# Fewer and larger first input transfers in a fused attention and soft-MoE kernel

## Chip, cores and metric

The kernel runs on one core of one Trainium2 chip. The metric is the device time of one launch in microseconds; lower is better.

## What is computed

An attention read between 512 tokens and 32 states for each of 8 batches and 8 heads (in both directions) is followed by a soft mixture of 8 experts with 4 slots each over all 4608 rows. Everything is float32. The reference, cut to its core:

```python
scores = scale * np.matmul(x, state.transpose(0, 1, 3, 2))       # x (8, 8, 512, 64), state (8, 8, 32, 64)
a = softmax(scores);   xread = np.matmul(a, state)
scores2 = scale * np.matmul(state, x.transpose(0, 1, 3, 2))
a2 = softmax(scores2); sread = np.matmul(a2, x)
x = np.concatenate([xread, sread], axis=2)                        # rows of 512 columns, 4608 of them
logits = x @ phi                                                  # phi (512, 32)
d = softmax(logits, axis=0); slot_input = d.T @ x
h = np.maximum(slot_input[e] @ w1[e], 0.0); slot_out[e] = h @ w2[e]
c = softmax(logits, axis=1); out = c @ slot_out
```

## The kernel before

One function, `attention_soft_moe`, writes the program. All loads and stores go through DMA queues, almost all through that of SyncE (SP). The tokens of one batch are 1 MB, `x0` to `x7`; the states (`stT_sb`, 512 KB) and the gate `phi_sb` (64 KB) are small; the weights `w1` and `w2` are 32 MB and follow behind the tokens on the same queue.

The first lines of the function issue the loads (lines 84 to 101). Batch 0 comes in four transfers of 256 KB, one for each pair of heads `g`: pieces 0 and 2 are issued by SP, pieces 1 and 3 by ScalarE (ACT). Then SP issues a quarter of the states (`st0`, batches 0 and 1), batch 1 in two halves, the other three quarters of the states (`st1`), `phi`, batches 2 to 7, and the weights. The semaphores that tell of a landing are eight, used in turn over all transfers of both queues, so a transfer may be issued only when the one eight before it has landed.

The order of the compute work is written out by hand in the table `ORDER` (lines 30 to 56), a list of steps such as `X.0.1`; each step is a small function of the same name. Those that matter here, for batch b:

- `W.n` (line 649): matmuls of the identity with itself, n columns, that keep TensorE (PE) busy while the first data is on its way.
- `X.b.g` (line 229): four PE transposes of 128x128 of token piece g into PSUM. `xe` (ACT, line 234) or `xd` (VectorE, DVE, line 239) copies the result to SBUF with the scale.
- `S.b` (line 248): 16 score matmuls from the transposed tokens and the states.
- `q`, `m1`, `sub`, `x1`, `l1`, `m2`, `e2` and so on: the softmaxes in both directions, on DVE, ACT and GpSimd (POOL).
- `G.i` (line 212): products of states and gate for two batches. Its operand `phi_bd` is built by two POOL copies from `phi_sb` (line 204), ahead of all other POOL work of the batches.

The table begins `W.512 W.256 X.0.1 xd.0.1 X.0.0 xd.0.0 X.0.2 xe.0.2 X.0.3 xe.0.3 S.0 X.1.0 m2.0.1 X.1.2 X.1.1 ... G.1 ... X.1.3 E.0.1 ... G.2 S.1`. Each engine works its share of the table in order. After the attention part (to about 76 us) come the expert matmuls with `w1` (line 700) and `w2` (line 763) and the output matmuls (lines 799 and 822), whose results ACT and DVE copy to SBUF and SP stores in 11 transfers.

The states' buffer is used a second time: when the last step that reads the states is through, `load_part` (line 686) puts a part of `w2` into it.

Of the kernel before, what the change touches and what calls it, by code (L numbers as in the profile page):

```python
# [8 lines left out]
F32 = mybir.dt.float32  # L9
# [6 lines left out]
P = 128  # L16
B = 8
S = 512
NS = 32
D = 64  # L20
E = 8
F = 1024
NJ = S // P
# [37 lines left out]


@with_exitstack
def attention_soft_moe(ctx: ExitStack, tc: tile.TileContext, x0, x1, x, st0, st1, phi, w1, w2a, w2b, out_x, out_s):

# [3 lines left out]
    nc = tc.nc  # L71
    pe, act, dve, pool = nc.tensor, nc.scalar, nc.vector, nc.gpsimd

    cp = ctx.enter_context(tc.tile_pool(name="const", bufs=1))
# [2 lines left out]
    pairs = ctx.enter_context(tc.tile_pool(name="pairs", bufs=NPAIR))  # L77


    one = ctx.enter_context(tc.tile_pool(name="one", bufs=1))  # L80
    stT_sb = one.tile([P, 4, 2, 2, 2, NS], F32, tag="one", name="stT_sb")
    phi_sb = cp.tile([P, 4, NS], F32, name="phi_sb")
    xb = []
    for b in range(B):
        t = big.tile([P, 4, NJ, 2 * D], F32, tag="big", name=f"x{b}")
        if b == 0:
            for i in range(4):
                v = x0[i].rearrange("p (g j c) -> p g j c", g=1, j=NJ)
                (act if i % 2 else nc.sync).dma_start(t[:, 1 * i : 1 * i + 1], v)
        elif b == 1:  # L90
            for i in range(2):
                v = x1[i].rearrange("p (g j c) -> p g j c", g=2, j=NJ)
                nc.sync.dma_start(t[:, 2 * i : 2 * i + 2], v)
        else:
            nc.sync.dma_start(t, x[b - 2].rearrange("p (g j c) -> p g j c", g=4, j=NJ))
        xb.append(t)
        if b == 0:
            nc.sync.dma_start(stT_sb[:, 0:1], st0)
        if b == 1:
            nc.sync.dma_start(stT_sb[:, 1:4], st1)  # L100
            nc.sync.dma_start(phi_sb, phi)


    w1t, w2t = {}, {}
# [34 lines left out]
    def load_part(t, k, e, ft):  # L139
        n = t.shape[1] // 256  # L140
        t = t.rearrange("p (k f) -> p k f", k=n)
        nc.sync.dma_start(t, w2a[e // 2, k][:, e % 2, ft : ft + n])
        for i in range(n):
            w2t[2, k, e, ft + i] = t[:, i]
# [32 lines left out]
    with ExitStack() as actx:  # L177
# [15 lines left out]
        def half(name):  # L193
            return wk.tile([P, S], F32, tag="h", name=name, bufs=NH)
# [487 lines left out]
        for i, step in enumerate(order):  # L682
            name, *args = step.split(".")
            steps[name](*map(int, args))
            if i == states_read:
                load_part(one.tile([P, F], F32, tag="one", name=f"w2_{k1}_{e1}"), k1, e1, 0)
            if i == halves_had:
                for k, e in ((k1, e1 + 1), (k2, e2)):
                    for ft in (0, 2):
                        load_part(half(f"w2_{k}_{e}_{ft}"), k, e, ft)  # L690
# [42 lines left out]
        c = [half(f"c{i}") for i in range(3)]  # L733
        c = [v[:, 0 : t.shape[1]].rearrange("p (t n) -> p t n", n=NS) for v, t in zip(c, c_t)]
# [213 lines left out]
```

## Time and profile before

| | us |
|---|---|
| median of 3 runs | 130.0 |
| lowest and highest run | 129.94, 130.71 |
| span of the profiled execution | 128.2 |

The profile tells the span of the profiled execution, from its first instruction to its last, and not that execution's device time. The difference to the median of the runs, 130.0 - 128.2 = 1.8 us, is taken as what lies around the span. All times inside the profile count from the start of the span.

In the rows, "PEld" is the loading of weights into PE, which overlaps the matmuls ("PE"); "SPq" and "ACTq" are DMA issues by SyncE and ScalarE. In brackets stands how long the engine sat idle before a group and what ended that. Matmul ends are modelled, so "PE busy" is an upper bound.

### The profile page before, as it was taken

The page shows a single profiled execution, that of the slowest core. Times are in us where ns is not written, and L with a number is a line of the kernel's source. Part 1 is how long each engine was busy: PE and PEld are TensorE (multiplying, and loading weights), DVE is VectorE, ACT ScalarE, POOL GpSimd, SP SyncE. Part 2 cuts the span into 40 slices and gives each one's busy share as a digit, 9 for nine tenths or more (in the row PEclk, how much of TensorE's full clock was granted, in tenths as well). Part 3 has the DMA queues.
Part 4 walks back from the last instruction along what each step waited for, and adds up shares of the span by engine and source line. Part 5 has one row for each costly group of instructions (what it writes and reads, how often), then busy time and mean ns, then how long its engine had stood idle before and what let it go on. Part 6 is the DMA issues. An engine that isn't in the chain of part 4 may idle for free.

```text
span 128.2 us, 4700 instructions
## 1 busy us (share of the span) xinstructions
PE 117.7 (92%) x1992; PEld 81.7 (64%) x1992; DVE 86.7 (68%) x194; ACT 76.9 (60%) x189; POOL 44.8 (35%) x63
## 2 busy tenths in 40 slices
PE   5999999999999999999999999999999999998600
PEld 2857686789795869768767769953465655575200
DVE  2329999999999999999985669019830356442600
ACT  4039999999999999999965711310100436645600
POOL 3004366391947467467882105703500000000000
PEclk9999999999999999999999999999999999999965
DMA  4999999999999999999999999999999989999992
GB/s 125 377 407 430 424 427 422 424 422 424 422 419 422 427 419 429 419 429 417 429 417 435 412 420 402 459 440 409 412 445 445 389 366 417 429 406 422 385 423 100
DMA packets 8373, 51.74 MB, mean 404 GB/s; under 512 B 928, under 2 KB 1184, under 8 KB 3360
## 3 DMA queue, kind: packets, MB, share of 16 engines
q1 hardware_dynamic: 8064, 50.93, 95.5%
q10 hardware_dynamic: 288, 0.52, 1.1%
q8 instruction: 15, 0.25, 0.7%
q14 instruction: 6, 0.05, 0.1%
HBM read 42.53 MB, written 8.91 MB: 401 GB/s over the span
## 4 chain that ended last, share of the span: by engine, by line
PE 71%; DVE 9%; DMA 7%; ACT 5%; issue 1%; POOL 0%; ACTq 0%; DVEq 0%; POOLq 0%
PE so_ps L763 12%; PE h_ps L700 11%; PE xt_ps L229 8%; PE o L799 7%; PE sc L248 5%; DMA phi_sb<-phi_in 5%; PE eT_ps L312 4%; PE sr_ps L346 4%; PE an_ps L312 3%; PE lt L381 3%; DMA x<-x_in 3%; PE t_ps L506 2%; DVE sums L277 2%; DVE q L261 2%; DVE m L266 1%
## 5 line engine op out<-in xcount | busy, mean ns | idle before, releaser
L270 POOL TENSOR_TENSOR q<-q,m 128x512 f32<-128x512 f32 x16 | 16.8, 1050 | 15.7 <-DVE m L266 7.3
L234 ACT ACTIVATE xt<-xt_ps 128x512 f32<-128x512 f32 x30 | 17.9, 618 | 5.9 <-PE xt_ps L229 5.7
L229 PE MATMUL xt_ps<-ident,x 128*128 128x128 f32 x128 | 19.3, 293 | 0.0
L288 POOL TENSOR_TENSOR q<-q,rr 128x512 f32<-128x512 f32 x16 | 16.5, 1051 | 5.1 <-DVE rr L283 3.6
L229 PEld LDWEIGHTS xt_ps<-ident,x 128*128 128x128 f32 x128 | 15.5, 151 | 3.1 <-PE sc L248 0.8
L763 PE MATMUL so_ps<-w,h_m 128*32 128x128 f32 (+1 forms) x384 | 15.7, 310 | 0.0
L763 PEld LDWEIGHTS so_ps<-w,h_m 128*32 128x32 f32 x384 | 10.7, 110 | 7.4 <-issue 4.6
L809 DVE COPY out<-o 128x512 f32<-128x512 f32 x14 | 9.2, 688 | 9.0 <-PE o L799 8.8
L700 PE MATMUL h_ps<-w,si_m 128*32 128x512 f32 x128 | 14.4, 594 | 0.1
L299 DVE TENSOR_REDUCE nm<-sc 128x1 f32<-128x512 f32 x16 | 10.6, 670 | 2.7 <-PE sc L248 2.7
L808 ACT COPY out<-o 128x512 f32<-128x512 f32 x14 | 7.7, 588 | 6.8 <-PE o L799 6.7
L700 PEld LDWEIGHTS h_ps<-w,si_m 128*32 128x32 f32 x128 | 9.1, 110 | 3.9 <-issue 2.9
L304 ACT ACTIVATE e<-sc,nm 128x512 f32<-128x512 f32 x16 | 11.3, 711 | 0.4 <-DVE nm L299 0.3
L261 DVE STREAM_TRANSPOSE q<-sc 128x512 f32<-128x512 f32 x16 | 11.1, 695 | 0.1
L293 DVE STREAM_TRANSPOSE aT<-q 128x512 f32<-128x512 f32 x16 | 10.9, 689 | 0.3 <-POOL q L288 0.2
L266 DVE TENSOR_REDUCE m<-q 128x16 f32<-128x512 f32 x16 | 10.5, 659 | 0.0
L277 DVE TENSOR_REDUCE sums<-q 128x16 f32<-128x512 f32 x16 | 10.4, 664 | 0.1
L273 ACT ACTIVATE q<-q 128x512 f32<-128x512 f32 x16 | 10.4, 650 | 0.1
L346 PE MATMUL sr_ps<-x,eT 128*32 128x64 f32 x512 | 10.4, 220 | 0.0
L312 PE MATMUL eT_ps<-ident,e 128*128 128x128 f32 x64 | 9.8, 279 | 0.0
L248 PE MATMUL sc<-xt,stT_sb 64*32 64x512 f32 x128 | 9.8, 601 | 0.0
L346 PEld LDWEIGHTS sr_ps<-x,eT 128*32 128x32 f32 x512 | 8.6, 110 | 1.3 <-issue 0.8
(124 smaller groups left out, 186.1 us busy)
## 6 DMA issues: line engine op xcount, KB each, us to landing
w<-w_in SPq DMA_DIRECT2D x16, 1024.0 KB, 19.7
w<-w2b_in SPq DMA_DIRECT2D x4, 2048.0 KB, 14.7
out_x<-out SPq DMA_DIRECT2D x7, 1024.0 KB, 6.0
x<-x_in SPq DMA_DIRECT2D x6, 1024.0 KB, 13.5
w<-w2a_in SPq DMA_DIRECT2D x6, 1024.0 KB, 19.4
x<-x_in SPq DMA_DIRECT2D x2, 512.0 KB, 5.9
w<-w2a_in SPq DMA_DIRECT2D x2, 512.0 KB, 12.4
w<-w2a_in SPq DMA_DIRECT2D x4, 256.0 KB, 14.4
```

The source lines that it names most:

```text
L229: pe.transpose(p[:, P * j : P * j + P], xb[b][:, g, j, :], ident)
L234: act.mul(r[f"xt{g}"], r[f"xp{g}"], 0.125)
L248: pe.matmul(r[f"sp{h}"][32 * g : 32 * g + 32, :], st_t(b, g)[64 * h : 64 * h + 64, :], r[f"xt{g}"][64 * h : 64 * h + 64, :], start=True, s ...
L261: dve.transpose(r[f"q{h}"], r[f"sp{h}"])
L266: dve.tensor_reduce(out=r[f"m1{h}"], in_=r[f"qv{h}"], axis=AX.X, op=ALU.max)
L270: pool.tensor_tensor(v, v, R[b][f"m1{h}"].broadcast_to([P, 16, NS]), op=ALU.subtract)
L277: dve.tensor_reduce(out=v, in_=R[b][f"qv{h}"], axis=AX.X, op=ALU.add)
L288: pool.tensor_tensor(v, v, r.broadcast_to([P, 16, NS]), op=ALU.mult)
L312: pe.transpose(p[:, j, :], r[f"{src}{h}"][:, P * j : P * j + P], ident)
L346: pe.matmul(r["srp"][32 * g : 32 * g + 32, h, :], r[f"eT{h}"][:, j, 32 * g : 32 * g + 32], xb[b][:, g, j, D * h : D * h + D], start=(j == ...
L700: pe.matmul(h_ps[hf][32 * kt : 32 * kt + 32, :], si_m[kt // 2][:, 256 * (kt % 2) + 32 * e : 256 * (kt % 2) + 32 * e + 32], w1t[hf, e, kt], ...
L763: pe.matmul(so[k][32 * i : 32 * i + 32, :], h_m[hf][:, 256 * i + 32 * e : 256 * i + 32 * e + 32], w(i), start=(hf == 0 and e == 0), stop=( ...
```

## The change

Batch 0 now comes in three transfers, all issued by SP: piece 1, piece 0 (256 KB each) and pieces 2 and 3 together (512 KB, a new input array `x0b`). ACT issues no load any more. The states and the gate share one tile `st_phi`: `phi` is appended to the rows of `st1` and comes with it in one transfer of 448 KB (line 100 of the new file). The later part of `w2` goes into the states' part of `st_phi`. Nine transfers ahead of batch 2 become seven. The steps and their order are unchanged; line numbers below line 89 fall by one.

```diff
--- before.py
+++ after.py
@@ -61,7 +61,7 @@
 
 
 @with_exitstack
-def attention_soft_moe(ctx: ExitStack, tc: tile.TileContext, x0, x1, x, st0, st1, phi, w1, w2a, w2b, out_x, out_s):
+def attention_soft_moe(ctx: ExitStack, tc: tile.TileContext, x0, x0b, x1, x, st0, st1, w1, w2a, w2b, out_x, out_s):
 
 
 
@@ -77,16 +77,16 @@
     pairs = ctx.enter_context(tc.tile_pool(name="pairs", bufs=NPAIR))
 
 
-    one = ctx.enter_context(tc.tile_pool(name="one", bufs=1))
-    stT_sb = one.tile([P, 4, 2, 2, 2, NS], F32, tag="one", name="stT_sb")
-    phi_sb = cp.tile([P, 4, NS], F32, name="phi_sb")
+    st_phi = cp.tile([P, F + 4 * NS], F32, name="st_phi")
+    stT_sb = st_phi[:, 0:F].rearrange("p (b g i c n) -> p b g i c n", b=4, g=2, i=2, c=2)
+    phi_sb = st_phi[:, F:].rearrange("p (g n) -> p g n", g=4)
     xb = []
     for b in range(B):
         t = big.tile([P, 4, NJ, 2 * D], F32, tag="big", name=f"x{b}")
         if b == 0:
-            for i in range(4):
-                v = x0[i].rearrange("p (g j c) -> p g j c", g=1, j=NJ)
-                (act if i % 2 else nc.sync).dma_start(t[:, 1 * i : 1 * i + 1], v)
+            for i in (1, 0):
+                nc.sync.dma_start(t[:, i : i + 1], x0[i].rearrange("p (g j c) -> p g j c", g=1, j=NJ))
+            nc.sync.dma_start(t[:, 2:4], x0b.rearrange("p (g j c) -> p g j c", g=2, j=NJ))
         elif b == 1:
             for i in range(2):
                 v = x1[i].rearrange("p (g j c) -> p g j c", g=2, j=NJ)
@@ -97,8 +97,7 @@
         if b == 0:
             nc.sync.dma_start(stT_sb[:, 0:1], st0)
         if b == 1:
-            nc.sync.dma_start(stT_sb[:, 1:4], st1)
-            nc.sync.dma_start(phi_sb, phi)
+            nc.sync.dma_start(st_phi[:, F // 4 :], st1)
 
 
     w1t, w2t = {}, {}
@@ -683,7 +682,7 @@
             name, *args = step.split(".")
             steps[name](*map(int, args))
             if i == states_read:
-                load_part(one.tile([P, F], F32, tag="one", name=f"w2_{k1}_{e1}"), k1, e1, 0)
+                load_part(st_phi[:, 0:F], k1, e1, 0)
             if i == halves_had:
                 for k, e in ((k1, e1 + 1), (k2, e2)):
                     for ft in (0, 2):
@@ -923,12 +922,13 @@
     xl = con(x.reshape(B, 4, 2, NJ, P, D).transpose(0, 4, 1, 3, 2, 5)).reshape(B, P, NJ * 8 * D)
     sl = con(state.reshape(4, 2, 2, 2, 2, NS, D).transpose(4, 6, 0, 3, 2, 1, 5)).reshape(P, 4, 2, 2, 2, NS)
     arrays = {
-        "x0_in": con(xl[0].reshape(P, 4, -1).transpose(1, 0, 2)),
+        "x0_in": con(xl[0].reshape(P, 4, -1).transpose(1, 0, 2)[0:2]),
+        "x0b_in": con(xl[0].reshape(P, 2, -1)[:, 1]),
         "x1_in": con(xl[1].reshape(P, 2, -1).transpose(1, 0, 2)),
         "x_in": con(xl[2:]),
         "st0_in": con(sl[:, 0:1]),
-        "st1_in": con(sl[:, 1:4]),
-        "phi_in": con(moe_phi.reshape(4, 2, D, NS).transpose(1, 2, 0, 3)).reshape(P, 4, NS),
+        "st1_in": con(_np.concatenate(
+            [sl[:, 1:4].reshape(P, -1), moe_phi.reshape(4, 2, D, NS).transpose(1, 2, 0, 3).reshape(P, 4 * NS)], axis=1)),
         "w1_in": con(moe_w1.reshape(E, 4, P, 2, 512).transpose(3, 0, 2, 1, 4)),
         "w2a_in": con(moe_w2[:, :, :256].reshape(E // 2, 2, 2, 4, P, 256).transpose(0, 2, 4, 1, 3, 5)),
         "w2b_in": con(moe_w2[:, :, 256:].reshape(E // 4, 4, 8, P, 2, P).transpose(0, 4, 3, 1, 2, 5)),
```

On SyncE's queue, the first transfers of the program; a row is line, operation, tile written and array read, shape. `DMAHW0` to `DMAHW7` are the eight landing semaphores, and a row that names one waits for the transfer that used it last. Before:

```order
L89 DMA x_71<-x_in 128x512 x2
L98 DMA stT_sb<-st_in 128x256
L93 DMA x_77<-x_in 128x1024 x2
L100 DMA stT_sb<-st_in 128x768
L101 DMA phi_sb<-phi_in 128x128 [waits DMAHW0_49]
L95 DMA x_82<-x_in 128x2048 [waits DMAHW1_49]
L95 DMA x_84<-x_in 128x2048 [waits DMAHW2_49]
```

After:

```order
L88 DMA x_67<-x_in 128x512 x2
L89 DMA x_67<-x0b_in 128x1024
L98 DMA st_phi<-st_in 128x256
L93 DMA x_72<-x_in 128x1024 x2
L100 DMA st_phi<-st_in 128x896
L95 DMA x_76<-x_in 128x2048
L95 DMA x_78<-x_in 128x2048 [waits DMAHW0_49]
```

One row more of batch 0 stands ahead of `st0`, and `phi` is gone as a row; the first row that waits for a landing is now batch 3's (for piece 1) and no longer `phi`'s.

On TensorE, the first steps behind the warm-up that wait for anything: `xt_ps_1` is `X.0.1`, `xt_ps_0` `X.0.0`, `xt_ps_2` and `xt_ps_3` the last two pieces of batch 0, `sc` `S.0`. Before:

```order
L229 MATMUL xt_ps_1_161<-ident,x_71 128x128 [waits DMAHW0_49]
...
L229 MATMUL xt_ps_0_168<-ident,x_71 128x128 [waits DMAHW1_49,PE_49]
...
L229 MATMUL xt_ps_2_175<-ident,x_71 128x128 [waits DMAHW3_49,PE_49]
...
L229 MATMUL xt_ps_3_182<-ident,x_71 128x128 [waits DMAHW2_49,DVE_49]
...
L248 MATMUL sc_0_189<-xt_0_173,stT_sb 32x512 [waits DMAHW4_49,DVE_49]
```

After:

```order
L228 MATMUL xt_ps_1_155<-ident,x_67 128x128 [waits DMAHW0_49]
...
L228 MATMUL xt_ps_0_162<-ident,x_67 128x128 [waits DMAHW1_49,PE_49]
...
L228 MATMUL xt_ps_2_169<-ident,x_67 128x128 [waits DMAHW2_49,PE_49]
...
L228 MATMUL xt_ps_3_176<-ident,x_67 128x128 [waits DVE_49]
...
L247 MATMUL sc_0_183<-xt_0_167,st_phi 32x512 [waits DMAHW3_49,DVE_49]
```

The order stays. `X.0.2` now waits for the third transfer (`DMAHW2`, 512 KB), and `X.0.3` no longer waits for a load of its own.

## Rows read from the trace of the kernel before

**Rows 1.** The page: span, and busy share of the DMA engines in 40 slices.

```profile
span 128.2 us, 4700 instructions
...
DMA  4999999999999999999999999999999989999992
```

**Rows 2.** The chain that ended last, first 14 us: start us, us, what.

```profile
0.73 3.30 DMA x<-x_in
...
4.04 5.99 DMA phi_sb<-phi_in
...
10.84 0.88 PE g_ps L212 x48
```

**Rows 3.** The same chain, a later pair of transpose steps.

```profile
20.84 0.87 PE xt_ps L229 x8
```

**Rows 4.** Timeline of the first 14 us: start us, us, engine, line, operation.

```profile
1.36 2.93 PE L649 MATMUL warm_ps<-ident 128*128 128x512 f32 x4 [1.36 <-POOL ident masks.py:199]
...
4.07 3.11 PEld L229 LDWEIGHTS xt_ps<-ident,x 128*128 128x128 f32 x16 [0.51 <-DMA x<-x_in]
4.08 3.34 PE L229 MATMUL xt_ps<-ident,x 128*128 128x128 f32 x16
...
6.93 1.12 ACT L234 ACTIVATE xt<-xt_ps 128x512 f32<-128x512 f32 x2 [3.99 <-PE xt_ps L229]
...
8.11 0.14 PEld L248 LDWEIGHTS sc<-xt,stT_sb 64*32 64x32 f32 x4 [0.39 <-ACT xt L234]
9.09 1.29 PEld L229 LDWEIGHTS xt_ps<-ident,x 128*128 128x128 f32 x12 [0.84 <-PE sc L248]
...
9.20 0.69 DVE L299 TENSOR_REDUCE nm<-sc 128x1 f32<-128x512 f32 x1 [2.43 <-PE sc L248]
...
10.84 0.72 PEld L212 LDWEIGHTS g_ps<-phi_bd,stT_sb 128*32 128x32 f32 x48 [0.46 <-POOL phi_bd L204]
...
12.56 0.62 ACT L234 ACTIVATE xt<-xt_ps 128x512 f32<-128x512 f32 x1
```

**Rows 5.** The same timeline, DMA issues alone.

```profile
0.73 0.89 ACTq L89 DMA_DIRECT2D x<-x_in  x2
...
0.74 0.85 SPq L89 DMA_DIRECT2D x<-x_in  x2
...
2.10 0.91 SPq L93 DMA_DIRECT2D x<-x_in  x2
...
3.05 0.43 SPq L100 DMA_DIRECT2D stT_sb<-st_in  x1
...
4.04 0.33 SPq L101 DMA_DIRECT2D phi_sb<-phi_in  x1
```

**Rows 6.** Single DMA issues: KB, us from issue to landing; order of issue.

```profile
x<-x_in ACTq DMA_DIRECT2D x1, 256.0 KB, 4.2
x<-x_in SPq DMA_DIRECT2D x1, 512.0 KB, 5.5
x<-x_in SPq DMA_DIRECT2D x1, 512.0 KB, 6.3
stT_sb<-st_in SPq DMA_DIRECT2D x1, 384.0 KB, 6.8
```

**Rows 7.** Windows: stretch, length, busy us of engines, granted clock, DMA share, GB/s.

```profile
0.00:2.85 2.85, 1.49 (x2) 0.84 (x3) 0.92 (x5) 1.20 (x1) 1.10 (x8) 1.00 0.34 88
0.00:3.50 3.50, 2.14 (x3) 1.11 (x4) 0.92 (x5) 1.28 (x1) 1.10 (x8) 1.00 0.47 147
0.00:4.85 4.85, 3.49 (x8) 1.96 (x9) 0.92 (x5) 1.28 (x1) 1.10 (x8) 1.00 0.63 216
10.00:20.00 10.00, 9.77 (x206) 7.11 (x204) 9.82 (x19) 9.84 (x23) 5.34 (x7) 1.00 1.01 425
119.00:120.00 1.00, 1.00 (x7) 0.30 (x4) 0.56 (x3) 0.67 (x3) 0.00 (x0) 1.00 0.71 295
```

**Rows 8.** What SyncE waited for, last store: us, times, longest.

```profile
SPq L940 <- DMA out_x<-out: 5.4, 1, 5.4
```

## Prediction

> **What bounds the kernel now.** I read the page first, then the chain that ended last, the timeline of the first 14 us, the DMA issues one by one, and windows of the start, the middle and the end.
>
> The page shows a span of 128.2 us in which the DMA engines are 90% busy or more in nearly every slice [rows 1]. So the first question is whether the end is set by the amount of data. It is not quite: in the window 119 to 120 us the DMA share falls to 0.71 [rows 7], because the loads are through by then and the stores wait for their results. The last store is waited for 5.4 us [rows 8], and it starts only when the last copy is done. What is saved on the compute path up to there moves the end by the same amount.
>
> In the middle the compute path is carried by DVE and ACT: from 10 to 20 us they are busy 9.82 and 9.84 of 10 us [rows 7]. Only what lets these two start their stream earlier is worth anything; what merely lets PE arrive earlier at a step that then waits for them is worth nothing.
>
> The chain begins with two DMAs: a piece of batch 0 (3.30 us from 0.73) and `phi` (5.99 us from 4.04), followed by `G.1` at 10.84 [rows 2]. Read alone, this says that two transfers hold up the start. The timeline corrects it at both places. First: the warm-up matmuls run from 1.36 for 2.93 us, that is to about 4.08 when the next one can start, and `X.0.1` starts at 4.08 [rows 4]. Its data landed at 0.73 + 3.30 = 4.03. Data and PE were ready together. Second: ahead of `G.1` the weight loads sat idle for 0.46 us behind the POOL copies of `phi` [rows 4], but DVE had begun at 9.20, released by the scores `S.0`, and ACT was in its stream too. Their start hangs on `S.0`, not on `phi`.
>
> So the path of the start is: warm-up to 4.08; 16 transposes in 3.34 us, to 7.42; the ACT copy of the last piece, for which the last score matmuls sat idle 0.39 us until 8.11; `S.0` through at about 9.1; then DVE at 9.20 and `X.1` at 9.09 [rows 4].
>
> The 16 transposes cost 3.34 / 16 = 0.209 us each; later 8 of them take 0.87, or 0.109 each [rows 3, 4]. The granted clock prints 1.00 in the first windows [rows 7], but a pitch twice as long is that of the lower of the clock's two levels, 1.2 instead of 2.4 GHz. What PE did before is the same warm-up in both kernels, so I take the same level for the same stretch.
>
> **The change part by part.** Against the span of 128.2 us:
>
> *Piece 1 alone at the head of one queue.* Before, pieces 0 and 1 moved side by side on two queues [rows 5]. By the windows, 88 x 2.85 = 251 KB had moved by 2.85 us, 147 x 3.5 = 515 KB by 3.5 and 216 x 4.85 = 1048 KB by 4.85 [rows 7]; all of batch 0 (1049 KB) had landed at about 1.17 + 4.2 = 5.4, ACT's second issue starting near 1.17 [rows 5, 6]. The lag from bytes to landing is about 0.55 us. If one queue moves the same bytes per time, piece 1 lands at 2.9 + 0.55 = 3.4, piece 0 at 4.1 and the 512 KB at 5.4. These are estimates from those rows. The first is 0.6 us earlier than now, but the warm-up holds PE until 4.08. What is left is that the first weight load, which now starts at 4.07, slips under the last warm-up matmul: 0.05 us, and at most 0.2, about the pitch of one transpose. At worst piece 1 comes as late as all of batch 0 did, at 5.4: a loss of 1.3. I take a gain of 0.05, since every row has the DMA engines near full from 3 us on.
>
> *Piece 0.* Needed at 4.08 + 4 x 0.209 = 4.92, there at about 4.1. Nothing.
>
> *Pieces 2 and 3 in one transfer.* `X.0.2` is needed at 4.08 + 8 x 0.209 = 5.75, and now has to wait for 512 KB, estimated at 5.4. The slack is 0.35 us, the smallest of all. The nearest row for 512 KB on SP is the first half of batch 1, 5.5 us from its issue [rows 6], but with twice the bytes ahead of it. From an issue at about 1.6 that would be 7.1, a loss of 7.1 - 5.75 = 1.35 us. I take nothing lost, and keep 1.35 as the end. The Trainium skill bears on this ("DMA: Bandwidth & Descriptors", section "Why a DMA increments its semaphore by 16 and not by 1"): a transfer counts as landed only when all the engines it runs on have reported, so the joined transfer holds back its first half until its second is there. No row here shows a joined transfer; by that rule the sum still stays at nothing while the slack of 0.35 lasts.
>
> *SP issues one transfer more ahead of batch 1.* Each takes some 0.43 us [rows 5], so batch 1 is issued 0.45 later. Its halves landed at 2.10 + 5.5 = 7.6 and about 2.58 + 6.3 = 8.9 [rows 5, 6], because of the bytes ahead of them and not because of their issue: the queue stays full. The same number of bytes is ahead of them now. `X.1` needs the first half at 9.09 and the second near 9.5. Nothing.
>
> *ACT issues nothing.* ACT loses 0.89 us of issuing at 0.73 [rows 5] and has its first copy at 6.93 [rows 4]. Nothing.
>
> *`phi` with `st1`.* They landed at 3.05 + 6.8 = 9.85 and 4.04 + 5.99 = 10.03 [rows 2, 5, 6]. So `phi`'s own transfer cost 0.18 us of a busy queue; its 65.5 KB at 425 GB/s [rows 7] are 0.15 of that. Joined, it lands some 0.03 us earlier, or a little more with the larger packets of batch 0. Even the whole 0.46 us of idle time ahead of `G.1` would mostly buy nothing: `S.1` behind it needs the copy of `X.1.3`, which ACT makes from 12.56 to 13.18 out of a stream without gaps [rows 4, 7]. I take 0, with 0 to 0.4 gain as bounds.
>
> *Issue waits and the second use of the states' buffer.* Batch 2 no longer waits for a landing before its issue, and batch 2 and everything behind it stands in a full queue. The part of `w2` is issued at the same place. Nothing.
>
> Sum: 0.05 gained, 128.15 us of span, and with the 1.8 us around it 129.95. I write 129.9.
>
> **The rivals.**
>
> A, *the 512 KB come late.* One queue starts slower than two, or the joined transfer waits for a slow engine, and `X.0.2` stands still. It decides from the point where the transfer lands after 5.75 us. For it: the first 2.85 us moved only 88 GB/s on average [rows 7], the start is the one stretch where the queues were not full, and the slack is only 0.35. Against it: the bytes that moved were limited by the engines' share soon after. Price up to 1.35 us: 131.3; a landing at 6.0 would give 130.2.
>
> B, *`phi` is a bound after all.* The chain names it. If it lands earlier and the streams of DVE and ACT follow through the POOL copies and `G.1`, up to 0.4 us is gained: 129.6. Against it: ACT and DVE start before `G.1`.
>
> C, *each transfer has a fixed price that shows.* The first transfer takes 3.30 us [rows 2] for 262 KB, which at 425 GB/s are 0.62; if 2.7 us of it were paid by each of the two transfers that go, 5.4 us are gained: 124.6. Against it speak `phi`'s 0.18 us behind `st1`. The Trainium skill has such a price ("DMA: Bandwidth & Descriptors", section "Anatomy of one DMA": about 2 us fixed per transfer, fitted on another issuing path). By that, two fewer would be worth 4 us; here transfers overlap, and the trace shows only 0.18 us between two landings.
>
> D, *the clock rises at another moment.* If all 16 transposes ran at 0.109, 16 x 0.100 = 1.6 us go: 128.3; if it rises as much later, 131.5. For it: the first transposes run at the low level, and the start of the data changes. Against it: PE does the same up to 4.08.
>
> **How the numbers follow.** A measurement of this kernel tells about 1% from no change. The forecast (within 0.3 us of no change) gets 0.74, A 0.08, B 0.12, C 0.01, D 0.05 in equal parts to both sides. Over 1% faster means under 128.7: C and the faster half of D, 0.04 with rounding up. Over 1% slower means above 131.3: the upper end of A and the slower half of D, 0.05. The rest, 0.91, lies within 1%. The range for 8 in 10 takes the spread of the runs (129.94 to 130.71), B's 129.6 with as much again below for its runs, and the part of A with a landing near 6.2: 129.2 to 130.8.
>
> **What would show it.** Right: `X.0.1` still starts at 4.08, without the idle time in front of its weight load; `X.0.2` near 5.75 and `X.0.3` wait for no DMA; DVE's first score reduction near 9.15; `G.1` still behind POOL. Wrong: idle time on PE with a DMA as its end between 4.1 and 7.4 (A), DVE's start unmoved but a shorter span (B), a pitch of 0.109 before 6.9 us or of 0.209 after it (D).

## The result: 0.6% slower

The changed kernel took 130.67 us (median of 22 runs) against 130.12 us for the kernel before (22 runs); the ratio is 1.006, with a 95% interval of 1.0038 to 1.0082. So it is slower, by less than the 1% that the prediction counted as a change, and on the side that was not forecast. The profiled execution has a span of 128.8 us against 128.2.

**The profile after.** The page, against [rows 1]:

```profile
span 128.8 us, 4698 instructions
...
DMA  4999999999999999999999999999999989999992
GB/s 122 277 425 428 433 420 428 417 430 422 425 417 430 417 425 422 422 428 415 430 420 428 417 419 401 442 438 438 402 440 433 417 333 428 420 419 421 388 426 109
```

The DMA engines are as full as before nearly everywhere, but the second value of the GB/s row, for 3.2 to 6.4 us, is only 277, where the page before has 377. The landings of single transfers, in the order of issue (KB, us from issue to landing), against [rows 6]:

```profile
x<-x_in SPq DMA_DIRECT2D x1, 256.0 KB, 2.7
x<-x_in SPq DMA_DIRECT2D x1, 256.0 KB, 2.9
x<-x0b_in SPq DMA_DIRECT2D x1, 512.0 KB, 5.3
st_phi<-st_in SPq DMA_DIRECT2D x1, 448.0 KB, 7.3
```

Pieces 1 and 0 landed at 0.74 + 2.7 = 3.4 and 1.17 + 2.9 = 4.1, as estimated. The joined 512 KB landed at 1.64 + 5.3 = 6.9, 1.5 us later than estimated, and the states with the gate at 3.52 + 7.3 = 10.8, against 10.0 before. The windows behind the second transfer (stretch, length, engines, granted clock, DMA share, GB/s) show where that went:

```profile
3.00:3.50 0.50, 0.50 (x2) 0.27 (x1) 0.00 (x0) 0.00 (x0) 0.00 (x0) 1.00 1.03 397
3.50:4.00 0.50, 0.50 (x2) 0.30 (x2) 0.00 (x0) 0.00 (x0) 0.00 (x0) 1.00 0.93 373
4.00:4.50 0.50, 0.50 (x3) 0.42 (x2) 0.00 (x0) 0.00 (x0) 0.00 (x0) 1.00 1.25 328
4.50:5.00 0.50, 0.50 (x7) 0.50 (x6) 0.08 (x1) 0.00 (x0) 0.00 (x0) 1.00 1.15 244
5.00:5.50 0.50, 0.32 (x3) 0.08 (x1) 0.50 (x1) 0.00 (x0) 0.00 (x0) 1.00 0.53 107
5.50:6.00 0.50, 0.00 (x0) 0.00 (x0) 0.50 (x2) 0.00 (x0) 0.00 (x0) 1.00 0.69 203
```

The kernel before, from 4.5 us on:

```profile
4.50:5.00 0.50, 0.50 (x5) 0.50 (x4) 0.00 (x0) 0.00 (x0) 0.00 (x0) 1.00 1.03 375
5.00:5.50 0.50, 0.50 (x4) 0.50 (x3) 0.28 (x1) 0.00 (x0) 0.00 (x0) 1.00 1.16 387
5.50:6.00 0.50, 0.50 (x4) 0.50 (x3) 0.42 (x1) 0.00 (x0) 0.00 (x0) 1.00 0.85 274
```

Up to 3.5 us the rate is near 400 GB/s, and between 3.5 and 4.0, right behind the first two transfers, still 373; then it sinks, to 107 between 5.0 and 5.5 us. Over the first 4.85 us the changed kernel moved 196 GB/s on average, or 951 KB, against 1048 KB before. So the joined transfer got under way in time, and its last part came late. The timeline of the first 14 us, against [rows 4]:

```profile
3.66 0.23 PEld L228 LDWEIGHTS xt_ps<-ident,x 128*128 128x128 f32 x1
4.08 1.24 PE L228 MATMUL xt_ps<-ident,x 128*128 128x128 f32 x8
...
7.02 1.06 PE L228 MATMUL xt_ps<-ident,x 128*128 128x128 f32 x8 [1.70 <-DMA x<-x0b_in]
...
9.92 0.69 DVE L298 TENSOR_REDUCE nm<-sc 128x1 f32<-128x512 f32 x1 [3.71 <-PE sc L247]
...
11.65 0.72 PEld L211 LDWEIGHTS g_ps<-phi_bd,st_phi 128*32 128x32 f32 x48 [0.56 <-POOL phi_bd L203]
```

The first weight load slipped under the warm-up (3.66), and the first eight transposes ran from 4.08. Then PE stood idle for 1.70 us until the joined transfer was there. `S.0` came through 0.7 us later (DVE starts at 9.92, before 9.20), and the weight loads of `G.1` started 0.8 us later (11.65, before 10.84), behind the POOL copies of the gate. The chain that ended last (start us, us, what) names the transfer of states and gate, as it named `phi` in [rows 2]:

```profile
3.52 7.33 DMA st_phi<-st_in
...
11.66 0.88 PE g_ps L211 x48
```

From here on the two traces run much alike. The first expert matmul starts 0.6 us later, and that is the difference of the spans. Before and after:

```profile
76.20 9.06 PE h_ps L700 x80
...
76.79 9.06 PE h_ps L699 x80
```

### The profile page after: what moved, and what is told of

It is laid out like the page before. It is cut to its first block, busy times and chain, and to the rows that moved or that the text cites. A ratio compares the mean times of both kernels' runs of the same rounds, so it can differ in the third digit from the quotient of the medians.

```text
span 128.8 us, 4698 instructions
## 1 busy us (share of the span) xinstructions
PE 116.5 (90%) x1992; PEld 80.5 (63%) x1992; DVE 86.5 (67%) x194; ACT 76.9 (60%) x189; POOL 44.8 (35%) x63
## 4 chain that ended last, share of the span: by engine, by line
PE 71%; DVE 9%; DMA 6%; ACT 4%; SPq 2%; issue 2%; POOL 0%; DVEq 0%; ACTq 0%; POOLq 0%
PE so_ps L762 12%; PE h_ps L699 11%; PE xt_ps L228 8%; PE o L798 7%; DMA st_phi<-st_in 6%; PE sc L247 5%; PE an_ps L311 4%; PE sr_ps L345 4%; PE eT_ps L311 4%; PE lt L380 3%; PE t_ps L505 2%; DVE sums L276 2%; DVE q L260 2%; DVE m L265 1%; PE sum_ps L786 1%
## 5 line engine op out<-in xcount | busy, mean ns | idle before, releaser
L228 PE MATMUL xt_ps<-ident,x 128*128 128x128 f32 x128 | 18.2, 279 | 1.7 <-DMA x<-x0b_in 1.7
L228 PEld LDWEIGHTS xt_ps<-ident,x 128*128 128x128 f32 x128 | 14.5, 143 | 4.6 <-issue 2.3
L247 PE MATMUL sc<-xt,st_phi 64*32 64x512 f32 x128 | 9.7, 601 | 0.0
```

Source lines behind the costliest of these rows:

```text
L228: pe.transpose(p[:, P * j : P * j + P], xb[b][:, g, j, :], ident)
L247: pe.matmul(r[f"sp{h}"][32 * g : 32 * g + 32, :], st_t(b, g)[64 * h : 64 * h + 64, :], r[f"xt{g}"][64 * h : 64 * h + 64, :], start=True, s ...
```

## The experiments

Four theories were tried first. "Join": the joined transfer is late by itself. "One queue": with everything on SyncE's queue the start is slower. "New array": the separate array `x0b` has slow first packets. "Phi": the gate joined with the states lands late and that sets the time. All ratios are to the kernel before, measured in the same jobs, with 95% intervals.

**Four pieces on SyncE's queue.** The changed kernel with

```diff
-            for i in (1, 0):
+            for i in (1, 0, 2, 3):
                 nc.sync.dma_start(t[:, i : i + 1], x0[i]...)
-            nc.sync.dma_start(t[:, 2:4], x0b...)
```

> The changed kernel, but batch 0 comes as four transfers of 256 KB, all on SyncE's queue in the order 1, 0, 2, 3, out of one array. In the profile of the changed kernel X.0.2 waited 1.70 us for the joined 512 KB, which landed near 6.9 us, and the DMA engines moved only 277 GB/s between 3.2 and 6.4 us. Theory 'join' (the joined transfer is what comes late): ratio to the kernel before 1.000 +- 0.002, X.0.2 without idle time for a DMA. Theory 'one queue' (two queues keep the engines busier at the start): ratio 1.004 to 1.008, X.0.2 or X.0.3 waits a microsecond or more. Theory 'new array' (the first packets out of a separate array are slow): 1.000. Theory 'phi' (the gate joined with the states lands late and that sets the time): 1.006.

Measured: 1.0039 (1.0018 to 1.006). The join alone is not the cause: without it some two thirds of the loss remain, and the two intervals overlap. The windows:

```profile
3.00:3.50 0.50, 0.50 (x2) 0.27 (x1) 0.00 (x0) 0.00 (x0) 0.00 (x0) 1.00 0.98 373
3.50:4.00 0.50, 0.50 (x2) 0.28 (x2) 0.00 (x0) 0.00 (x0) 0.00 (x0) 1.00 0.09 29
4.00:4.50 0.50, 0.50 (x5) 0.42 (x4) 0.00 (x0) 0.00 (x0) 0.00 (x0) 1.00 0.67 184
4.50:5.00 0.50, 0.50 (x7) 0.45 (x5) 0.21 (x1) 0.00 (x0) 0.00 (x0) 1.00 0.94 295
```

The rate falls to 29 GB/s between 3.5 and 4.0 us, right when the first two transfers (512 KB) are through, though the third had been issued at 1.63 us. This is one execution. Another kernel below has the same transfers (four pieces on SyncE's queue, with the gate steps moved); in its profile there is no such gap, and `X.0.2` does not wait:

```profile
3.50:4.00 0.50, 0.50 (x2) 0.30 (x2) 0.00 (x0) 0.00 (x0) 0.00 (x0) 1.00 1.09 348
...
4.08 3.23 PE L227 MATMUL xt_ps<-ident,x 128*128 128x128 f32 x16
```

The timeline of the kernel with the gap has a second lesson:

```profile
6.04 1.27 PE L227 MATMUL xt_ps<-ident,x 128*128 128x128 f32 x8 [0.86 <-DMA x<-x_in]
...
9.10 0.69 DVE L297 TENSOR_REDUCE nm<-sc 128x1 f32<-128x512 f32 x1 [3.02 <-PE sc L246]
...
11.50 0.71 PEld L210 LDWEIGHTS g_ps<-phi_bd,st_phi 128*32 128x32 f32 x48 [0.99 <-POOL phi_bd L202]
```

`X.0.2` waited 0.86 us, but its eight transposes took 1.27 us (the eight of [rows 4] took 0.209 each), and DVE began at 9.10, no later than before. The weight loads of `G.1` came at 11.50, 0.7 us late, and the span was still 129.0. The first expert matmul starts at 76.68 there, 0.5 us later than before; the other 0.3 us of the span came behind it.

**Joined, out of one array.** The changed kernel with `x0b` replaced by `x0[2:4]` of a four-piece array.

> The changed kernel, but the 512 KB transfer reads pieces 2 and 3 out of the same array as pieces 0 and 1, so each row of it is two runs of 2 KB instead of one of 4 KB. 'Join': 1.006, X.0.2 waits about 1.7 us. 'One queue': 1.006. 'New array': 1.000, no packet stall at the third transfer. 'Phi': 1.006.

Measured: 1.0039 (1.001 to 1.0069); `X.0.2` waited 0.83 us, half of what "join" expected. "New array" falls. In this profile `G.1` came as late as in the changed kernel, and DVE began at 9.45, but the span is only 128.3:

```profile
11.65 0.72 PEld L211 LDWEIGHTS g_ps<-phi_bd,st_phi 128*32 128x32 f32 x48 [0.95 <-POOL phi_bd L203]
```

**The joined transfer on ScalarE's queue.**

```diff
-            nc.sync.dma_start(t[:, 2:4], x0b...)
+            act.dma_start(t[:, 2:4], x0b...)
```

> The changed kernel, but the 512 KB transfer is issued by ScalarE at the start, beside pieces 1 and 0 on SyncE's queue. 'One queue': about 1.000, X.0.2 waits less than 0.3 us. 'Join': 1.004 or more, as the joined transfer still has to land whole. 'New array': 1.006, the stall stays. 'Phi': 1.006.

Measured: 1.0059 (1.0026 to 1.0091). A second queue alone does not mend it. In the profiled execution (131.89 us, above the kernel's median of 131.03) another thing is late:

```profile
5.06 3.72 PE L228 MATMUL xt_ps<-ident,x 128*128 128x128 f32 x16 [0.78 <-DMA x<-x_in]
```

`X.0.1` itself waits until 5.06. Piece 1 is on its way together with 512 KB that are needed later; in this execution also no byte moved between 2.0 and 2.5 us, where the changed kernel had 156 GB/s. Which of the two makes piece 1 late, and whether it makes the ratio, is not shown.

**The gate joined, nothing else.** The kernel before with `st_phi` and one transfer for `st1` and `phi`.

> The kernel before, with the gate joined to the three quarters of the states in one transfer and one tile, and nothing else: batch 0 in four pieces on two queues. 'Phi': 1.006. 'Join', 'one queue' and 'new array': 1.000 +- 0.002, G.1 at the same time as before or up to 0.1 us earlier.

Measured: 0.999 (0.9971 to 1.001). This half of the change is free. "Phi" falls as the cause. `G.1` was expected at the same time or 0.1 us earlier; in the profile it came 0.4 us later (11.20), at no cost.

So the loss comes from the way batch 0 is brought in. A theory that fits the gap in the windows: the third transfer of a queue does not follow its first two at once, and whatever it is comes late. Before, each queue's first two transfers were batch 0, 1 MB in all, and SyncE's third was `st0`.

**Two joined transfers on SyncE's queue.** Pieces 0 and 1, then 2 and 3:

```diff
-            for i in (1, 0):
-                nc.sync.dma_start(t[:, i : i + 1], x0[i]...)
-            nc.sync.dma_start(t[:, 2:4], x0b...)
+            for i in range(2):
+                nc.sync.dma_start(t[:, 2 * i : 2 * i + 2], x0[i]...)
```

> The changed kernel, but batch 0 comes as two transfers of 512 KB on SyncE's queue (pieces 0 and 1, then 2 and 3): one queue, joined transfers, and the queue's third transfer is now the states, after 1 MB. With four pieces on one queue the DMA engines had run almost empty from 3.5 to 4.0 us, right behind the second transfer. Theory 'third transfer' (the queue's third transfer is not ready when the first two are done, and two transfers of 256 KB last too short to cover it): no gap at 3.5 to 4.0, all of batch 0 landed by about 5.5, X.0.2 waits less than 0.3 us, ratio 0.998 to 1.002. Theory 'time' (something slows all transfers from 3.5 to 6 us, whichever they are): second transfer late, near 6.5, ratio 1.004. Theory 'join' (a joined transfer is late by itself): ratio 1.004 or more.

Measured: 1.0006 (0.9986 to 1.0025). One queue and two joined transfers, and no loss clear of the noise. The second transfer landed at 1.17 + 4.3 = 5.5:

```profile
x<-x_in SPq DMA_DIRECT2D x1, 512.0 KB, 4.3
```

The windows show a slow stretch too, but behind the first megabyte, where the states and batch 1 move, and with the engines busy (a DMA share of 0.91 to 1.14, where the gap above has 0.09):

```profile
3.50:4.00 0.50, 0.50 (x2) 0.06 (x1) 0.00 (x0) 0.00 (x0) 0.00 (x0) 1.00 1.01 385
...
4.50:5.00 0.50, 0.50 (x4) 0.50 (x3) 0.00 (x0) 0.00 (x0) 0.00 (x0) 1.00 0.92 322
5.00:5.50 0.50, 0.50 (x5) 0.50 (x4) 0.21 (x1) 0.00 (x0) 0.00 (x0) 1.00 1.14 260
5.50:6.00 0.50, 0.50 (x4) 0.50 (x3) 0.48 (x1) 0.00 (x0) 0.00 (x0) 1.00 0.91 213
```

So neither the single queue nor the join costs by itself, which fits the theory that what counts is what the queue's third transfer carries. `G.1` started 0.5 us later than before (11.33) at no cost.

**Piece 1 on ScalarE's queue.** The changed kernel with `(act if i else nc.sync)` for pieces 1 and 0; the joined transfer is then the second on SyncE's queue.

> The changed kernel, but piece 1 is issued by ScalarE, so SyncE's queue holds piece 0, the joined 512 KB and then the states. 'Third transfer': the third one of SyncE's queue comes behind 768 KB and the joined transfer is its second; batch 0 landed by about 5.5, X.0.2 waits less than 0.3 us, ratio 0.998 to 1.002. 'Time' or 'join': X.0.2 waits 0.8 us or more, ratio 1.004 to 1.006.

Measured: 0.9973 (0.9952 to 0.9995), and in a second measurement (below) 0.9968 (0.993 to 1.0006). The joined transfer landed 4.3 us from its issue instead of 5.3:

```profile
x<-x0b_in SPq DMA_DIRECT2D x1, 512.0 KB, 4.3
```

The 16 transposes run as one group of 2.48 us, with no wait for the joined transfer, and DVE starts at 8.50:

```profile
4.19 2.48 PE L228 MATMUL xt_ps<-ident,x 128*128 128x128 f32 x16
...
8.50 0.69 DVE L298 TENSOR_REDUCE nm<-sc 128x1 f32<-128x512 f32 x1 [2.07 <-PE sc L247]
...
11.21 0.72 PEld L211 LDWEIGHTS g_ps<-phi_bd,st_phi 128*32 128x32 f32 x48 [0.94 <-POOL phi_bd L203]
```

The early start of DVE is for the most part not the doing of the transfers: the 16 transposes took 2.48 us here and 3.34 before. In the profile of the second measurement they took 3.37 us and DVE began at 9.30, later than before:

```profile
4.15 3.37 PE L228 MATMUL xt_ps<-ident,x 128*128 128x128 f32 x16
```

**Pairs by queue.** Pieces 1 and 0 on SyncE's queue, 2 and 3 on ScalarE's.

> The changed kernel with four pieces of 256 KB: 1 and 0 on SyncE's queue, 2 and 3 on ScalarE's. Two transfers of batch 0 on each queue as in the kernel before, but pieces 0 and 1 share a queue. 'Third transfer': batch 0 landed by about 5.4, ratio 0.998 to 1.002, X.0.1 starts near 4.1. 'Time': pieces 3 and 0 late, ratio 1.004.

Measured: 1.0003 (0.9986 to 1.002). Two transfers of batch 0 per queue, and no loss, though in its profile DVE began 0.4 us later than before (9.61), with `G.1` at 10.96.

**Piece 1 cut in two.** The changed kernel with piece 1 as two transfers of 128 KB, so that piece 0 is the third.

> The changed kernel with piece 1 cut into two transfers of 128 KB (two of its four row blocks each), all on SyncE's queue. 'Third transfer': the gap moves forward, to about 2.9 us behind 256 KB, piece 0 (now the third) lands after 4.6 instead of 4.06, X.0.0 waits, ratio 1.005 to 1.010. 'Time': piece 0 lands near 4.1 as in the changed kernel and the joined transfer near 6.9; ratio 1.006 either way, so the place of the gap tells, not the ratio.

Measured: 1.0123 (1.0085 to 1.0162). The gap moved forward, to 147 GB/s between 3.0 and 3.5 us, behind the first 256 KB:

```profile
2.50:3.00 0.50, 0.50 (x2) 0.21 (x1) 0.00 (x0) 0.00 (x0) 0.00 (x0) 1.00 1.25 322
3.00:3.50 0.50, 0.50 (x2) 0.27 (x1) 0.00 (x0) 0.00 (x0) 0.00 (x0) 1.00 0.59 147
3.50:4.00 0.50, 0.50 (x2) 0.29 (x2) 0.00 (x0) 0.00 (x0) 0.00 (x0) 1.00 1.22 418
```

and piece 0, the third transfer, landed at 1.63 + 3.8 = 5.4 instead of 4.1:

```profile
x<-x_in SPq DMA_DIRECT2D x1, 256.0 KB, 3.8
```

So where a gap was seen, it moved with the end of the second transfer: at 3.0 us behind 256 KB and at 3.5 behind 512. This speaks for a late third transfer, but does not show it. In the changed kernel the rate stays at 373 GB/s right behind the second transfer and sinks a microsecond later; the same four pieces showed a gap in one profile and none in another; and the slow stretch of the two joined transfers has busy engines. What the ratios show is where batch 0 must not be: in the third or a later transfer of SyncE's queue it cost 0.4 to 1.2% (four kernels), and in the first two of each queue nothing, but for the joined transfer on ScalarE's queue. A rival stands untested: each of these transfers but one has 128 rows, so what goes with the number of transfers could as well go with the number of rows in the queue. Why the engines wait is not shown either.

**The gate steps moved behind S.1.** To see whether the late gate costs by itself, the four `G` steps were put behind `S.1` in the table, in four kernels:

```diff
-... q.0.0 G.1 xe.1.2 G.0 m2.0.0 G.3 m1.0.0 X.1.3 E.0.1 e2.0.0 xe.1.3 q.0.1 sub.0.0 x1.0.0 m1.0.1 G.2 S.1 ...
+... q.0.0 xe.1.2 m2.0.0 m1.0.0 X.1.3 E.0.1 e2.0.0 xe.1.3 q.0.1 sub.0.0 x1.0.0 m1.0.1 S.1 G.1 G.0 G.3 G.2 ...
```

In the changed kernel:

> The changed kernel with the four G steps taken from between X.1.1 and S.1 and put right behind S.1, so that on TensorE no batch step ahead of S.1 stands behind the landing of the gate. In the profile of the changed kernel S.0 was 0.7 us and G.1 0.8 us later than before. Theory 'two gates' (the late S.0 and the late gate each carry about half of the loss): ratio 1.001 to 1.004. Theory 'S.0 alone': 1.006, as the changed kernel.

With piece 1 on ScalarE's queue:

> The kernel with piece 1 on ScalarE's queue (0.9973 of the kernel before), with the four G steps behind S.1. 'Two gates': 0.993 to 0.996, as G.1 stood 0.7 us idle there. 'S.0 alone': 0.997.

In the kernel before:

> The kernel before with the four G steps behind S.1 and nothing else. G.1 stood 0.23 us idle (0.46 us for the weight loads) in its profile. 'Two gates': 0.997 to 0.999. 'S.0 alone': 1.000.

With four pieces on SyncE's queue:

> Four pieces of 256 KB on SyncE's queue (1.0039 of the kernel before; in its profile DVE began at 9.10 us, not later than before, while G.1 was 0.66 us later), with the four G steps behind S.1. 'Two gates': 0.998 to 1.001. 'S.0 alone': 1.004.

Measured, in this order: 1.0117 (1.0092 to 1.0142), 1.0088 (1.0055 to 1.012), 1.0074 (1.0046 to 1.0102), 1.0073 (1.0044 to 1.0102). All are slower, the kernel before too, so the move costs some 0.7% by itself and neither theory had that. Why is not shown. Set against each other, the four pieces on one queue lose nothing more than the kernel before does (1.0073 and 1.0074), which would fit a loss by the gate alone; but the changed kernel still loses 0.4% more (1.0117 and 1.0074), which would fit a loss by the scores. The intervals are wider than the 0.004 in question, and in the profile of the four pieces batch 0 was hardly late. Inconclusive.

**The gate alone late.** The kernel before, with `phi` issued behind the first half of batch 2:

```diff
-            nc.sync.dma_start(phi_sb, phi)
...
+            if b == 2:
+                nc.sync.dma_start(t[:, 0:2], v[:, 0:2])
+                nc.sync.dma_start(phi_sb, phi)
+                nc.sync.dma_start(t[:, 2:4], v[:, 2:4])
```

> The kernel before, with the gate's transfer put behind the first half of batch 2 (512 KB, so it should land some 1.2 us later, near 11.2); batch 0 and all ahead of it as before. 'Two gates' (a late gate by itself costs about half of its delay): ratio 1.003 to 1.006, G.1 near 12.0. 'S.0 alone': 0.999 to 1.001.

Measured: 1.029 (1.0251 to 1.0329), far more than either theory said.

```profile
9.46 0.69 DVE L304 TENSOR_REDUCE nm<-sc 128x1 f32<-128x512 f32 x1 [2.67 <-PE sc L253]
...
13.55 0.72 PEld L217 LDWEIGHTS g_ps<-phi_bd,stT_sb 128*32 128x32 f32 x48 [2.57 <-POOL phi_bd L209]
```

DVE starts at 9.46, 0.26 us later than before, and `G.1` waits 2.57 us and starts 2.7 us later. The gate landed later than planned (8.3 us from its issue at 4.44), and the price is more than its delay: the span is 132.4, 4.2 us longer. A gate that is 2.7 us late costs, by itself. But not all of the price is the wait: `G.1`'s matmuls ended 2.33 us of idle time on PE, and from 14.28 to 17.70 the granted clock is 0.50, the lower level, where the kernel before has 1.00.

```profile
14.28:17.70 3.42, 3.42 (x44) 2.21 (x40) 1.28 (x2) 1.81 (x4) 1.36 (x2) 0.50 1.02 431
```

Half of that stretch, 1.7 us, is an estimate of what the clock took at most. In the changed kernel the clock did not fall there, so this run does not tell what a gate 0.8 us late costs.

**The scores alone late.** The kernel before with one more `W.512` between `X.0.0` and `X.0.2`.

> The kernel before, with one more warm-up matmul of 512 columns between X.0.0 and X.0.2, which makes S.0 and DVE's start some 0.5 to 1 us later while the gate lands as before. 'Two gates': half of that delay, ratio 1.002 to 1.004. 'S.0 alone': the whole of it, 1.004 to 1.008.

Measured: 1.0035 (0.9995 to 1.0074). It tells the theories apart no further: in its profile DVE began at 9.22, so the added matmul did not delay the scores in that execution as meant; the 16 transposes took 1.47 + 1.04 us instead of 3.34 and made up for it.

**The states on ScalarE's queue too.** The kernel with piece 1 on ScalarE's queue, and

```diff
-            nc.sync.dma_start(stT_sb[:, 0:1], st0)
+            act.dma_start(stT_sb[:, 0:1], st0)
```

> The kernel with piece 1 on ScalarE's queue and piece 0 and the joined 512 KB on SyncE's (0.9973 of the kernel before), with the first quarter of the states moved to ScalarE's queue too. 'Third transfer': the third one of SyncE's queue is now the first half of batch 1; batch 0 stays on time, ratio 0.995 to 0.999. If the states beside the joined transfer hold it back by 0.3 us or more: 0.999 to 1.001.

Measured: 0.996 (0.9928 to 0.9992), the lowest ratio of all, though not told apart from the kernel without this edit (0.9973 and 0.9968), with a span of 127.8:

```profile
span 127.8 us, 4698 instructions
```

```profile
5.82 1.06 PE L228 MATMUL xt_ps<-ident,x 128*128 128x128 f32 x8 [0.44 <-DMA x<-x0b_in]
...
8.72 0.69 DVE L298 TENSOR_REDUCE nm<-sc 128x1 f32<-128x512 f32 x1 [2.45 <-PE sc L247]
...
10.77 0.71 PEld L211 LDWEIGHTS g_ps<-phi_bd,st_phi 128*32 128x32 f32 x48 [0.87 <-POOL phi_bd L203]
```

`X.0.2` still waits 0.44 us here: PE was through with the first eight transposes at 5.4, and the joined transfer landed at 1.17 + 4.5 = 5.7, 0.2 us later than without this edit. `G.1` starts at 10.77, 0.44 us ahead of the kernel without it.

**Piece 1 on ScalarE's queue, again.**

> The kernel with piece 1 on ScalarE's queue, unchanged, a second time: 0.995 to 0.9995 again if its gain over the kernel before is real; 0.9995 or above if the first measurement was at the edge of its noise.

Measured: 0.9968 (0.993 to 1.0006). The same size of gain as the first time; the interval just reaches no change.

## Why the prediction was wrong

*What bounds the kernel.* Right that the start decides and that what is lost there comes out at the end: 0.6 us at the first expert matmul, 0.6 us of span. Right also that DVE's start hangs "on `S.0`, not on `phi`": with the gate alone late it began at 9.46, long before `G.1`. Wrong was to conclude that the gate's landing has no price: 2.7 us late, it cost 4.2 us of span, a fall of the clock included. Whether the 0.8 us by which the gate was late in the changed kernel is part of its loss stays open. For it: with four pieces on one queue the span grew by 0.8 us in an execution whose scores were not late. Against it: with the joined transfer out of one array `G.1` was just as late and the span grew by 0.1, and where `G.1` was 0.3 to 0.5 us late (11.20, 11.33, 11.21 and 11.10) nothing was lost.

*Piece 1 and piece 0.* Right in the landings: 3.4 and 4.1 estimated and measured. The first weight load slipped under the warm-up as expected (3.66 instead of 4.07), but the first transpose starts at 4.08 in both kernels, so the gain of 0.05 us does not show.

*The clock.* "The same level for the same stretch" did not hold: the first eight transposes took 1.24 us, or 0.155 each, against 0.209 [rows 4], after the same warm-up, and the last eight 1.06. This differs between executions of one kernel (2.48 and 3.37 us for all 16 with piece 1 on ScalarE's queue), so it need not be an effect of the change. The gain of 0.4 us on the first eight was eaten by the wait that followed.

*Pieces 2 and 3 in one transfer.* This is the step that failed. The estimate of 5.4 us rested on "if one queue moves the same bytes per time", and the cost was taken as "nothing lost". The transfer landed at 6.9, near the 7.1 that I had kept as the far end, and PE waited 1.70 us. The bytes came as estimated up to 3.5 us, and by 4.85 us 951 KB had moved where the prediction had 1048; what failed is the rest, at 244, 107 and 203 GB/s from 4.5 to 6.0 us, against 375, 387 and 274 before. The runs showed that batch 0 loses its time when part of it is in the third or a later transfer of SyncE's queue: 1.006, 1.0039, 1.0039 and 1.0123, against 1.0006 with two joined transfers on that queue and 1.0003 with two and two. The prediction had only rows in which two queues' first two transfers covered batch 0. Why the rate falls stays open. The rule of the Trainium skill that the prediction cites there ("DMA: Bandwidth & Descriptors", section "Why a DMA increments its semaphore by 16 and not by 1"), that a transfer counts as landed only when all its engines have reported, fits the longer wait of `X.0.2`: 1.70 us for the joined transfer and 0.86 for piece 2 alone. These are two executions, and with the joined transfer as its queue's second nothing is lost, so its share is not shown.

*More issues ahead of batch 1.* "Nothing" came out, but not for the reason given, that the queue stays full: the first half of batch 1 landed at 2.58 + 5.9 = 8.5 instead of 7.6, and `X.1`, itself late, did not need it before 9.80.

*`phi` with `st1`.* Right that the join is free (0.999). But it landed 0.8 us later than before in the changed kernel and 0.4 us of delay at `G.1` came with the join alone, where the prediction had a landing 0.03 us earlier.

*The rivals.* A happened, at its place (`X.0.2`) and beyond its point of decision (5.75 us). Its mechanism was only half right: the start was as fast as before, 87 GB/s over the first 2.85 us against 88, and the slow stretch came later. Its price was below the 1.15 us that go with a landing at 6.9, because the last eight transposes took 1.06 us instead of 1.67. In that execution this was luck. B came true in part and with the other sign: a gate late enough is a bound. C fell. D happened in part, in our favour. A sign that A deserved more than 0.08 stood in the kernel before: its rate, too, falls behind batch 0, to 274 GB/s from 5.5 to 6.0 us, so the queue was not full throughout.

## What to carry to other kernels

Count the transfers on each queue before the first data is needed. Here it cost 0.4 to 1.2% to have part of that data in the third or a later transfer of one queue, and nothing to have it in two large transfers on that queue, or in two on each of two queues: the same four pieces took 1.0039 on one queue and 1.0003 as two and two. When the chain of waits names a load, test its landing by delaying it alone before arguing that the wait is covered, and look at the granted clock in that run, because a long wait can cost more than itself. A stall seen in one profile is worth looking for in a second one of the same transfers before it is called a property of them.

## What was not expected of the hardware

Behind a queue's second transfer the DMA engines could fall far below their rate, with more transfers long issued: 29 GB/s from 3.5 to 4.0 us with four pieces on one queue, 147 from 3.0 to 3.5 with the first piece cut. It did not happen in every execution: the same four pieces showed 348 GB/s from 3.5 to 4.0 us in another profile, and the changed kernel fell only later, to 107 from 5.0 to 5.5. What makes the engines wait stays open. A small transfer of 64 KB that set `G.1` 2.7 us late cost 4.2 us of span, with the granted clock at 0.50 for 3.42 us after PE had stood idle.
